# Attention products on half-height tiles, and a local and a strided group taken together

## The chip, the cores and the metric

The kernel runs on one core of a Trainium2 chip. The metric is the device time of one execution in microseconds (us). Before the change it is 878.13 us, the median of 3 runs (877.97 to 878.93).

## The reference

The program computes sparse attention and then a feed-forward layer on its result. There are 8 images of 8 heads, 576 tokens and 64 values per head.

```python
scores = scale * np.matmul(q, k.transpose(0, 1, 3, 2))
mask_local = (rel >= 0) & (rel < stride)            # heads 0 to 3, stride 32
mask_strided = (rel >= 0) & (pos[None, :] % stride == pos[:, None] % stride)   # heads 4 to 7
scores = np.where(masks[None, :, :, :], scores, -1000000000.0)
...
attn = attn / (np.sum(attn, axis=-1, keepdims=True) + 1e-09)
x = (attn @ v) in rows of tokens, 4608 x 512
h = x @ w_in                                       # 512 -> 2048
return ((h * (1.0 / (1.0 + np.exp(-h)))) @ w_out)  # 2048 -> 512
```

A local head sees the 32 tokens up to its own, a strided head the tokens at its own place modulo 32, at most 18 of them. So each score matrix is a set of small blocks.

## The kernel before

**The feed-forward layer.** Each fp32 operand is split in two fp32r parts, and three of the four products are formed on TensorE. A product of this kind has 128 rows of weights, 128 weight columns and 512 moving columns; the text calls it a big product. The first three blocks of 512 tokens are computed directly (`hidden` at L591, `output` at L638). The last six blocks go in three pairs with a Strassen scheme of seven products (L1386 for the hidden layer, L1424 for the output), whose weight operands are formed during blocks 1 and 2 (`prepare`) and kept in DRAM.

**The attention.** A head pair lies in the 128 partitions. Its blocks are cut into six groups per image: three local ones of 12 tiles (32 query rows, 64 keys) and three strided ones of 8, 8 and 6 tiles (64 rows that hold three residues of 18 tokens). A group goes through these steps, with the letters that the planner uses:

- S, scores (L440): one fp32 matmul per tile over all 128 partitions. Its moving operand is `kbd`, which holds the keys of one head beside zeros and zeros beside the other's, so that 2 x 64 columns come out for the two heads.
- M (`peak`, L456, VectorE): mask, scale and row maximum, two instructions for each column of 128 queries. A local group has 3 such columns, a strided one 4, 4 or 3.
- E (L465, ScalarE): the exponential with its row sum, also two for each column. For the first images it is one subtraction on GpSimd (U) and one exponential.
- R (`total`), the reciprocal of the sums, and for strided groups N (`scale`, L489), the scaling of the weights, both on VectorE.
- T (L495): the transposes on TensorE, then P (L499), ScalarE's copy out of PSUM.
- O, values: L507 for local groups (result with queries in the partitions) and L515 for strided ones (result with the head's values in the partitions), with `vbd`, again a block next to zeros.
- Local groups then take Q (`share`, L525, scaling on VectorE) and B, the turn into columns of x: 16 transposes of 32 x 96 on VectorE (L561), or for images 0 and 1 transposes on TensorE (X, L545) and a copy. Strided groups are copied by ScalarE (L538).

**PSUM.** In blocks 0 to 2 the pool `ps` has 4 buffers of one bank, shared by the attention and the hidden layer, and `ps_o` 4. In the Strassen pairs the attention has the 2 buffers of `ps1`, the products `z` 6 banks.

**The order of work.** A planner in the file (class `Steps`) sets the order of the instructions on each engine. Each step has a cost on the engines that may run it, rings of buffers that it takes, and a due time. `arrange` places step by step the one that can start first, and among those that can start within 0.05 us of it the one with the earliest due time. Image 0 comes before the feed-forward layer. Image 1 runs during block 0 on due times of its own. The groups of the other images run at places in a table: `burst(c)` puts T of group c + 1, S of group c + 2 and O of group c at one place.

Of the kernel before, what the change touches and what calls it, by code (L numbers as in the profile page):

```python
# [26 lines left out]
STRIDE = 32  # L27
# [19 lines left out]
KBUFS = 2  # L47
VBUFS = 2
# [25 lines left out]
class Group:  # L74
    def __init__(self, local, first, count):
        self.local, self.first, self.count = local, first, count
        self.rows = STRIDE if local else KW
        self.per = P // self.rows
        self.n = count // self.per
        step = STRIDE if local else SEQ  # L80
        self.q0 = [step * t for t in range(count)]
        half = S // STRIDE
        gap = [STRIDE if local and first < half <= first + t else 0 for t in range(count)]
# [156 lines left out]
def sparse_attention_ffn(ctx: ExitStack, tc: tile.TileContext, kqt, vt, w_in, w_out, out, out_t):  # L240
# [8 lines left out]
    ps = early.enter_context(tc.tile_pool(name="ps", bufs=8 - NTT, space=PSUM))  # L249
    ps_o = early.enter_context(tc.tile_pool(name="ps_o", bufs=NTT, space=PSUM))  # L250
    banks = {"att": ps}
# [5 lines left out]
        (1, 0, 9): "vbd2", (1, 1, 9): "zeros", (1, 0, 7): "kbd2",  # L257
# [6 lines left out]
    vbds = [const.tile([P, 2, VT * D], F32, name=f"vbd{i}") for i in range(VBUFS + 1)]  # L264
    kbds = [const.tile([P, 3, QW], F32, name=f"kbd{i}") for i in range(KBUFS + 1)]
    const.tile([P, 64], F32, name="pad1")
    zeros = const.tile([P, VT * D], F32, name="zeros")
# [5 lines left out]
    nc.vector.memset(kbds[0][:, 0], 0.0)  # L273
    nc.gpsimd.memset(kbds[0][:, 2], 0.0)
    nc.vector.memset(kbds[1][:, 0:3:2], 0.0)
    nc.vector.memset(vbds[0], 0.0)
    nc.vector.memset(zeros, 0.0)
    nc.vector.memset(kbds[2][:, 0:3:2], 0.0)
    for vbd in vbds[1:]:
        for h in range(2):  # L280
            nc.scalar.copy(out=vbd[:, h], in_=zeros)
    vbds = [vbd.rearrange("p h (t d) -> p h t d", d=D) for vbd in vbds]


# [107 lines left out]
    def load_qk(b, gi):  # L392
        n = max(GROUPS[gi].nq, GROUPS[gi].nk)
        for h in range(2):
            load(out=kbds[gi % (KBUFS if b else KBUFS + 1)][h::2, h : h + 2, :n],
                 in_=kqt[b, gi, h::2, :, :n])

    def load_v(b, gi):
        n = GROUPS[gi].count
        for h in range(2):  # L400
            load(out=vbds[gi % (VBUFS if b else VBUFS + 1)][h::2, h, :n], in_=vt[b, gi, h::2, :n])

# [9 lines left out]

    class Attention:


        def __init__(self, b, gi):
            self.b, self.gi, self.g = b, gi, GROUPS[gi]
            g = self.g
            self.kbd = kbds[gi % (KBUFS if b else KBUFS + 1)]
            self.vbd = vbds[gi % (VBUFS if b else VBUFS + 1)]  # L420
            self.cols = g.n * P
            self.tiles = [
                (t, t // g.per, slice(t % g.per * g.rows, (t % g.per + 1) * g.rows))
                for t in range(g.count)
            ]

            self.quick = NG * b + gi < 2 * NG + 2

        def bank(self, name):

            if self.b == 0 and name != "pss":
                return ps_o.tile([P, 512], F32, name="po")
            return banks["att"].tile([P, 512], F32, name="ps")

        def scores(self):
            g, kbd = self.g, self.kbd
            self.pss = self.bank("pss")
            s_ps = self.pss.rearrange("p (c h k) -> p c h k", h=2, k=KW)
            for t, c, rows in self.tiles:
                nc.tensor.matmul(  # L440
                    s_ps[rows, c], kbd[:, 1, g.q0[t] : g.q0[t] + g.rows],
                    kbd[:, 0:3:2, g.k0[t] : g.k0[t] + KW], start=True, stop=True,
                )

        def peak(self):
            g = self.g
            s_ps = self.pss.rearrange("p (c h k) -> p c h k", h=2, k=KW)
            self.sm = att.tile([P, 512], F32, name="sm", bufs=3)
            self.s_sb = s_sb = self.sm.rearrange("p (c k h) -> p c h k", h=2, k=KW)
            sums = att.tile([P, 4, 4, 2], F32, name="sums", bufs=4)  # L450
            self.nmax, self.rsum = nmax, rsum = sums[:, 0], sums[:, 1]
            self.inv = rsum[:, : g.n].unsqueeze(3).broadcast_to([P, g.n, 2, KW])
            for c in range(g.n):
                for h in range(2):

                    nc.vector.tensor_tensor_reduce(  # L456
                        out=s_sb[:, c, h], in0=s_ps[:, c, h],
                        in1=masks[g.local, g.starts[c]][:, :KW],
                        scale=-SCALE, scalar=BIG, op0=ALU.add, op1=ALU.min,
                        accum_out=nmax[:, c, h : h + 1],  # L460
                    )

        def exp_one(self, c):
            for h in range(2):
                nc.scalar.activation(  # L465
                    out=self.s_sb[:, c, h], in_=self.s_sb[:, c, h], func=AF.Exp,
                    bias=self.nmax[:, c, h : h + 1], scale=-1.0,
                    accum_out=self.rsum[:, c, h : h + 1],
                )

        def below(self):
            s_sb = self.s_sb[:, : self.g.n]
            peak = self.nmax[:, : self.g.n].unsqueeze(3).broadcast_to([P, self.g.n, 2, KW])
            nc.gpsimd.tensor_sub(s_sb, peak, s_sb)

        def exp(self):
            sm = self.sm[:, : self.cols]
            nc.scalar.activation(out=sm, in_=sm, func=AF.Exp)

        def total(self):  # L480
            rsum, s_sb = self.rsum[:, : self.g.n], self.s_sb[:, : self.g.n]
            if self.quick:
                nc.vector.tensor_reduce(out=rsum, in_=s_sb, op=ALU.add, axis=mybir.AxisListType.X)
# [3 lines left out]
        def scale(self):  # L487
            s_sb = self.s_sb[:, : self.g.n]
            nc.vector.tensor_mul(s_sb, s_sb, self.inv)  # L489

        def turn(self):
            self.psp = self.bank("psp")
            for c in range(self.g.n):
                at = slice(c * P, (c + 1) * P)
                nc.tensor.transpose(self.psp[:, at], self.sm[:, at], ident)  # L495

        def turned(self):
            self.pt = att.tile([P, 512], F32, name="pt")
            nc.scalar.copy(out=self.pt[:, : self.cols], in_=self.psp[:, : self.cols])  # L499

        def values(self):
            g, pt, vbd = self.g, self.pt, self.vbd
            self.pso = pso = self.bank("pso")
            if g.local:
                o_ps = pso.rearrange("p (c h d) -> p c h d", h=2, d=D)
                for t, c, rows in self.tiles:
                    nc.tensor.matmul(  # L507
                        o_ps[rows, c], pt[:, c * P + rows.start : c * P + rows.stop], vbd[:, :, t],
                        start=True, stop=True,
                    )  # L510
                return
            for t, c, rows in self.tiles:
                p0 = c * P + rows.start
                for h in range(2):
                    nc.tensor.matmul(  # L515
                        pso[h * D : (h + 1) * D, t * SEQ : (t + 1) * SEQ], vbd[:, h, t],
                        pt[:, p0 : p0 + SEQ], start=True, stop=True,
                    )

        def share(self):  # L520
            g = self.g
            self.xq = att.tile([P, 3 * P], F32, name="xq", bufs=1)
            o_ps = self.pso.rearrange("p (c h d) -> p c h d", h=2, d=D)
            o_sb = self.xq.rearrange("p (c h d) -> p c h d", h=2, d=D)
            nc.vector.tensor_mul(o_sb[:, : g.n], o_ps[:, : g.n], self.inv)  # L525

        def sorted(self):
            g, pso = self.g, self.pso

            places = STRIDE + 1  # L530
            at, end = 3 * g.first, 3 * (g.first + g.count)
            while at < end:
                hp, r = divmod(at, places)
                n = min(end - at, STRIDE - r)
                s0 = at - 3 * g.first
                src = pso[:, s0 * NJ : (s0 + n) * NJ].rearrange("p (r j) -> p r j", j=NJ)
                dst = place_of(self.b)[:, NP // 2 + hp].rearrange("p (j r) -> p r j", r=STRIDE)
                nc.scalar.copy(out=dst[:, r : r + n], in_=src)  # L538
                at += n + (r + n == STRIDE)

        def back(self):
            self.psx = self.bank("psp")
            for c in range(self.g.n):
                at = slice(c * P, (c + 1) * P)
                nc.tensor.transpose(self.psx[:, at], self.xq[:, at], ident)  # L545

        def done(self):
            flat = place_of(self.b).rearrange("p n s -> p (n s)")
            x0 = self.g.first * STRIDE
            nc.scalar.copy(out=flat[:, x0 : x0 + self.cols], in_=self.psx[:, : self.cols])  # L550

        def blocks_of(self, t):

            g, n = self.g, P // STRIDE
# [1078 lines left out]
```

## Time and profile before

| what | value |
| --- | --- |
| median of the runs | 878.13 us |
| the profiled execution | 881.13 us |
| its span, first to last instruction | 879.3 us |
| granted TensorE clock | 0.994 |
| busy: TensorE, VectorE, ScalarE, GpSimd | 852.1, 615.0, 467.0, 119.3 us |
| DMA | 180.32 MB, 205 GB/s on average |

The page gives for each engine its busy time and for groups of instructions the busy time, the mean of one, the idle time before them and what ended it. A matmul of two fp32 operands stands in the trace as two products. Lines such as L440 are lines of the kernel printed above.

### The profile page before, as it was taken

Reading aid. Unit: us, or ns where it says so; the run is one execution under the profiler, and the core shown is the slowest. Engines: PE = TensorE matmul, PEld = TensorE weight load, DVE = VectorE, ACT = ScalarE, POOL = GpSimd, SP = SyncE. Lnnn points to the kernel's source line nnn. Section 1 sums busy time; section 2 is a strip of 40 time slices with the busy share of each in tenths; the row PEclk is TensorE's granted clock in tenths of the full one; section 3 lists DMA queues with packets and bytes.
Section 4 is the critical chain, followed back from the end, with each engine's and each line's share of the span. In section 5 each row is a group of like instructions: output and inputs, shape, how many; then the busy total and the mean of one; then the engine's idle time right before and its main releaser. Section 6 shows DMA issues by size and latency. Waiting matters only on the chain.

```text
span 879.3 us, 15187 instructions
## 1 busy us (share of the span) xinstructions
PE 852.1 (97%) x5554; PEld 684.6 (78%) x5554; DVE 615.0 (70%) x1608; ACT 467.0 (53%) x1006; POOL 119.3 (14%) x136
## 2 busy tenths in 40 slices
PE   6799999999999999999999999999999999999997
PEld 4677777778878878777788777787888878888886
DVE  7899757984896797738399975935895660178662
ACT  4888554445456445456754654647554434455440
POOL 4000115332444335200000000000000000000000
PEclk9899999999999999999999999999999999999999
DMA  7897886666444455555655765764546565554562
GB/s 220 297 289 244 241 254 211 226 207 191 141 141 171 140 189 185 189 204 201 228 193 183 244 218 194 259 231 165 194 153 252 194 234 212 196 192 150 218 244 107
DMA packets 79626, 180.32 MB, mean 205 GB/s; under 512 B 7872, under 2 KB 56000, under 8 KB 68800
## 3 DMA queue, kind: packets, MB, share of 16 engines
q1 hardware_dynamic: 79552, 179.35, 60.1%
q8 instruction: 44, 0.72, 0.3%
q14 instruction: 30, 0.25, 0.1%
HBM read 140.53 MB, written 38.80 MB: 204 GB/s over the span
## 4 chain that ended last, share of the span: by engine, by line
PE 73%; DVE 13%; DMA 7%; ACT 3%; POOL 2%; issue 2%; SPq 0%; POOLq 0%; ACTq 0%; DVEq 0%
PE z L1386 26%; PE z L1424 25%; PE po L638 7%; PE ps L591 7%; PE ps L440 4%; DMA stage<-w_in 2%; PE ps L515 2%; DMA w<-ops 2%; DVE g L618 2%; DVE xb L561 2%; DVE w L561 1%; PE ps L495 1%; DVE sm L456 1%; DVE th L605 1%; DMA kbd<-kqt 1%
## 5 line engine op out<-in xcount | busy, mean ns | idle before, releaser
L1386 PE MATMUL z<-w,w 128*128 128x512 f32 x720 | 168.5, 392 | 1.4 <-DMA w<-ops 0.7
L1386 PEld LDWEIGHTS z<-w,w 128*128 128x128 f32 x720 | 134.2, 188 | 31.4 <-issue 1.1
L1424 PE MATMUL z<-w,w 128*128 128x512 f32 x576 | 136.3, 391 | 0.5 <-DMA w<-ops 0.5
L591 PE MATMUL ps<-xhi,w 128*128 128x512 f32 x384 | 131.1, 399 | 2.3 <-ACT pt L499 1.4
L1424 PEld LDWEIGHTS z<-w,w 128*128 128x128 f32 x576 | 107.4, 188 | 24.0 <-DMA w<-ops 1.0
L591 PEld LDWEIGHTS ps<-xhi,w 128*128 128x128 f32 x384 | 72.0, 188 | 21.0 <-issue 1.7
L465 ACT ACTIVATE sm<-sm,sums 128x64 f32<-128x64 f32 x228 | 77.3, 345 | 15.3 <-DVE sums L456 15.2
L591 PE MATMUL ps<-xlo,w 128*128 128x512 f32 x192 | 75.0, 391 | 0.2 <-DVE xlo L583 0.2
L638 PE MATMUL po<-w,g 128*128 128x512 f32 x276 | 71.2, 393 | 0.5 <-DVE g L618 0.4
L638 PEld LDWEIGHTS po<-w,g 128*128 128x128 f32 x276 | 51.2, 188 | 12.6 <-DVE g L618 2.1
L601 ACT ACTIVATE th<-ps 128x512 f32<-128x512 f32 x48 | 28.6, 596 | 49.5 <-PE ps L591 35.3
L440 PE MATMUL ps<-kbd 128*32 128x128 f32 (+1 forms) x928 | 48.4, 294 | 6.5 <-POOL mask_strided L287 5.6
L561 DVE STREAM_TRANSPOSE xb<-xq 32x96 f32<-32x96 f32 x192 | 51.7, 269 | 3.0
L1424 PE MATMUL z<-xhi,w 128*128 128x512 f32 x216 | 52.6, 392 | 0.0
L1424 PE MATMUL z<-xlo,w 128*128 128x512 f32 x216 | 52.6, 392 | 0.0
L1255 DVE TENSOR_TENSOR w<-w,w 128x1024 fp32r<-128x1024 f32 (+3 forms) x41 | 44.9, 1105 | 8.2 <-ACT w L1326 8.1
L440 PEld LDWEIGHTS ps<-kbd 128*32 128x32 f32 (+1 forms) x928 | 35.5, 126 | 18.7 <-issue 10.3
L961 POOL TENSOR_TENSOR stage<-w,w 128x512 f32<-128x512 f32 x23 | 34.7, 1512 | 96.3 <-DMA ops<-stage 70.7
L1424 PEld LDWEIGHTS z<-xlo,w 128*128 128x128 f32 x216 | 40.2, 188 | 8.8 <-issue 0.5
L1424 PEld LDWEIGHTS z<-xhi,w 128*128 128x128 f32 x216 | 40.1, 188 | 8.4 <-issue 0.2
L605 DVE SCALAR_TENSOR_TENSOR th<-th,ps 128x512 f32<-128x512 f32 x48 | 32.5, 677 | 19.1 <-ACT th L601 18.9
L618 DVE TENSOR_TENSOR g<-th,g 128x512 fp32r<-128x512 f32 x48 | 43.8, 912 | 1.7 <-ACT g L614 0.8
(172 smaller groups left out, 1459.0 us busy)
## 6 DMA issues: line engine op xcount, KB each, us to landing
w<-ops SPq DMA_DIRECT2D x84, 1024.0 KB, 4.8
ops<-stage SPq DMA_DIRECT2D x64, 256.0 KB, 2.3
vbd<-vt SPq DMA_DIRECT2D x48, 192.0 KB, 3.6
ops<-w SPq DMA_DIRECT2D x65, 128.0 KB, 3.8
stage<-w_in SPq DMA_DIRECT2D x16, 512.0 KB, 5.2
stage<-w_out SPq DMA_DIRECT2D x16, 512.0 KB, 5.5
kbd<-kqt SPq DMA_DIRECT2D x32, 221.0 KB, 3.9
kbd<-kqt SPq DMA_DIRECT2D x32, 208.0 KB, 3.2
```

The costliest lines, as they stand in the source:

```text
L440: nc.tensor.matmul(s_ps[rows, c], kbd[:, 1, g.q0[t] : g.q0[t] + g.rows], kbd[:, 0:3:2, g.k0[t] : g.k0[t] + KW], start=True, stop=True,)
L465: nc.scalar.activation(out=self.s_sb[:, c, h], in_=self.s_sb[:, c, h], func=AF.Exp, bias=self.nmax[:, c, h : h + 1], scale=-1.0, accum_out ...
L561: nc.vector.transpose(out=dst[cols, :, rows], in_=src[rows, :, cols])
L591: nc.tensor.matmul(ph, weight(0, wi, fc)[:, cc * P : (cc + 1) * P], x[xi][:, cc], start=(cc, n) == (0, 0), stop=(cc, n) == (NP - 1, 2),)
L601: nc.scalar.activation(out=th[:, cols], in_=ph[:, cols], func=AF.Tanh, scale=0.5)
L605: nc.vector.scalar_tensor_tensor(out=th[:, cols], in0=th[:, cols], scalar=1.0, in1=ph[:, cols], op0=ALU.add, op1=ALU.mult,)
L618: nc.vector.tensor_sub(out=g[1][:, cols], in0=th[:, cols], in1=g[0][:, cols].bitcast(F32))
L638: nc.tensor.matmul(po[tt], g[gi][:, cols], weight(1, wi, fc), start=fc == 0 and n == 0, stop=fc == NFC - 1 and n == 2,)
L961: nc.gpsimd.tensor_add(raw[:, 2 * n : 2 * n + 2].rearrange("p a q -> p (a q)"), weight(layer, 0, fc).bitcast(F32), weight(layer, 1, fc).bi ...
L1255: nc.vector.tensor_tensor(out=o, in0=x, in1=y, op=op1)
L1386: nc.tensor.matmul(zt[z][:, jj], w[:, at, wi, cc * P : (cc + 1) * P], op[:, xi, cc], start=fresh and (cc, n) == (0, 0), stop=(cc, n) == (1 ...
L1424: nc.tensor.matmul(zt[zz][:, ds], w[:, at, wi, ds * P : (ds + 1) * P], op[:, gi, jj], start=fresh and (jp, jj, n) == (0, 0, 0), stop=(jp, ...
```

## The change

Each head's product stands alone on 64 rows of the array, head 0 in partitions 0 to 63 and head 1 in 64 to 127, so the zeros beside the blocks and the instructions that wrote them are gone (`kds`, `vds`, three buffers each). The values are formed with the head's values in the partitions, for local groups too; two index bits per product choose the half of the array (`r`) and the half of the result (`r ^ b`), and the host turns the halves of q, k and v to match. ScalarE copies the result straight into x, so `share`, `back`, `done` and `blocks_of` go, and the weights of local groups are scaled before the values as those of strided groups are.

For images 1 to 7 a local and a strided group form one step of 7 (or 6) columns. Scores, transposes and values take the new pool `ps_a`: one buffer of two banks, one bank for each head or each group. The hidden layer keeps 2 buffers, the output 4 banks. The places of S, T and O in the table are now apart from each other. A second `upper` buffer is added in `prepare`, and three weight tiles that shared memory with `kbd`, `vbd` and `zeros` have their own.

```diff
-KBUFS = 2
-VBUFS = 2
+KBUFS = 3
+VBUFS = 3
...
-    ps = early.enter_context(tc.tile_pool(name="ps", bufs=8 - NTT, space=PSUM))
-    ps_o = early.enter_context(tc.tile_pool(name="ps_o", bufs=NTT, space=PSUM))
+    ps_a = ctx.enter_context(tc.tile_pool(name="ps_a", bufs=1, space=PSUM))
+    ps = early.enter_context(tc.tile_pool(name="ps", bufs=6 - NTT, space=PSUM))
+    ps_o = early.enter_context(tc.tile_pool(name="ps_o", bufs=NTT // 2, space=PSUM))
...
         def scores(self):
-            for t, c, rows in self.tiles:
-                nc.tensor.matmul(
-                    s_ps[rows, c], kbd[:, 1, g.q0[t] : g.q0[t] + g.rows],
-                    kbd[:, 0:3:2, g.k0[t] : g.k0[t] + KW], start=True, stop=True,
-                )
+            for g, c0, k in zip(self.gs, self.c0, self.k):
+                kd = kds[k]
+                for t in range(g.count):
+                    rows = slice(t % g.per * g.rows, (t % g.per + 1) * g.rows)
+                    at = (c0 + t // g.per) * KW
+                    for r in range(2):
+                        half = slice(r * D, (r + 1) * D)
+                        nc.tensor.matmul(
+                            self.pss[rows, r, at : at + KW],
+                            kd[half, 1, g.q0[t] : g.q0[t] + g.rows],
+                            kd[half, 0, g.k0[t] : g.k0[t] + KW], start=True, stop=True,
+                        )
...
         def values(self):
+            for g, c0, v in zip(self.gs, self.c0, self.v):
+                wide = STRIDE if g.local else SEQ
+                for t in range(g.half):
+                    for b in range(2):
+                        tile_ = b * g.half + t
+                        q0 = c0 * P + tile_ * g.rows
+                        for r in range(2):
+                            half, to = (slice(x * D, (x + 1) * D) for x in (r, r ^ b))
+                            at = base + t * wide
+                            nc.tensor.matmul(
+                                self.pso[to, b, at : at + wide], vds[v][half, tile_],
+                                self.pt[half, q0 : q0 + wide], start=True, stop=True,
+                            )
...
+        def placed(self, i):
+            if g.local:
+                nc.scalar.copy(
+                    out=flat[:, x0 : x0 + 2 * n].rearrange("p (b n) -> p b n", b=2),
+                    in_=self.pso[:, :, base : base + n],
+                )
...
-    groups = [Attention(b, gi) for b in range(B) for gi in range(NG)]
+    groups = [Attention(0, (gi,)) for gi in range(NG)]
+    groups += [Attention(b, (gi, gi + NG // 2)) for b in range(1, B) for gi in range(NG // 2)]
...
-    for i, at in enumerate([(1, fc) for fc in (0, 2, 4, 5, 7, 9, 11, 12, 14)]
-                           + [(2, fc) for fc in (0, 1, 3, 5, 6, 8, 9, 11, 12)]):
-        plan[at] = 2 * NG + i
+    for i in range(3 * NG // 2):
+        for what, c, at in (("V", i, 3.55 * i), ("T", i + 1, 3.55 * i + 1.2), ("S", i + 2, 3.55 * i + 2.4)):
+            k, fc = divmod(int(at), NFC)
+            plan.setdefault((k + 1, fc), []).append((what, ahead + c))
```

How the order of the instructions changes is shown at three places. A row names the line, the operation, what it writes and reads, the shape, and how often it stands in a row.

TensorE in the first Strassen pair, before: L1386 are big products, L495 transposes, L440 scores, L507 values of a local group.

```order
L1386 MATMUL z<-w_4_4062,w_9_3960 128x512 x24
L495 MATMUL ps<-ident,sm 128x128 x3
L440 MATMUL ps<-kbd_82 32x128 x12
L1386 MATMUL z<-w_8_4058,w_12_4145 128x512 x12
L507 MATMUL ps<-vbd_79,pt 32x128 x12
...
L495 MATMUL ps<-ident,sm 128x128 x3
L440 MATMUL ps<-kbd_83 64x128 x8
L1386 MATMUL z<-xhi,w_5_4258 128x512 x12
L507 MATMUL ps<-vbd_80,pt 32x128 x12
```

The same place now: L1325 are big products, L481 transposes, L425 scores, L503 values.

```order
L1325 MATMUL z<-w_8_4196,w_12_4364 128x512 x24
L481 MATMUL pa<-ident,sm 128x128 x7
L1325 MATMUL z<-xhi,w_5_4517 128x512 x24
L425 MATMUL pa<-kd_83 32x64 x24
L425 MATMUL pa<-kd_84 64x64 x12
L1325 MATMUL z<-w_0_3431,w_9_4549 128x512 x24
L503 MATMUL pa<-pt,vd_87 64x32 x24
L503 MATMUL pa<-pt,vd_85 64x54 x16
L1325 MATMUL z<-w_4_4217,w_12_4573 128x512 x24
```

Scores and values of a local and a strided group now stand together, with twice as many matmuls for each group, half as many moving columns, and 24 big products between neighbouring steps where 12 stood.

VectorE in block 1, before, behind the scores of a local group: L456 is M, L525 is Q, L484 and L485 are R, L561 the transposes into x.

```order
L456 ISA sm,sums<-ps,mask_local 128x64
L456 ISA sums 128x1
L525 TENSOR_TENSOR xq<-ps,sums 128x384
L484 TENSOR_SCALAR sums<-sums 128x6
L485 RECIPROCAL sums<-sums 128x6
L561 STREAM_TRANSPOSE xb<-xq 32x3x32 x12
L456 ISA sm,sums<-ps,mask_strided 128x64
```

VectorE in block 1 now, behind the scores of a pair: L443 is M, L577, L586 and L590 belong to the hidden layer, L470 and L471 are R, L474 is N.

```order
L443 ISA sm,sums<-pa,mask_strided 128x64
L443 ISA sums 128x1
L577 SCALAR_TENSOR_TENSOR th<-th,ph 128x512
L586 CAST g<-th 128x512
L590 TENSOR_TENSOR g<-th,g 128x512
L470 TENSOR_SCALAR sums<-sums 128x14
L471 RECIPROCAL sums<-sums 128x14
L577 SCALAR_TENSOR_TENSOR th<-th,ph 128x512
L474 TENSOR_TENSOR sm<-sm,sums 128x896
```

The scaling of the values and the transposes are gone; one R and one N serve both groups.

TensorE at the start, image 0, before: the letters are those above, L545 is X.

```order
L440 MATMUL ps<-kbd_82 32x128 x12
L440 MATMUL ps<-kbd_83 32x128 x12
L440 MATMUL ps<-kbd_84 32x128 x12
L495 MATMUL po<-ident,sm 128x128 x6
L507 MATMUL po<-vbd_79,pt 32x128 x12
L440 MATMUL ps<-kbd_82 64x128 x8
L545 MATMUL po<-ident,xq 128x128 x3
```

The start now:

```order
L425 MATMUL pa<-kd_82 32x64 x24
L425 MATMUL pa<-kd_83 32x64 x24
L425 MATMUL pa<-kd_84 32x64 x24
L425 MATMUL pa<-kd_82 64x64 x16
L481 MATMUL po<-ident,sm 128x128 x6
L503 MATMUL po<-pt,vd_85 64x32 x24
L425 MATMUL pa<-kd_83 64x64 x16
```

Image 0 keeps its six single groups; the fourth group's scores come ahead of the first transposes, all scores share the one buffer of `pa`, and the turn back (X) is gone.

More of the change, by code (lines that the diff above doesn't have):

```diff
@@ L82, in __init__ @@
         half = S // STRIDE
-        gap = [STRIDE if local and first < half <= first + t else 0 for t in range(count)]
+        self.half = count // 2
+        gap = [STRIDE if local and t >= self.half else 0 for t in range(count)]
         self.k0 = [q0 + g for q0, g in zip(self.q0, gap)]
@@ L411, in place_of, with __init__ @@
         return xs[b]
+    turn_k, turn_v = itertools.count(), itertools.count()
     class Attention:
[L416 to L427, printed above, removed]
+        def __init__(self, b, gis):
+            self.b, self.gis = b, gis
+            self.gs = [GROUPS[gi] for gi in gis]
+            self.c0 = [sum(g.n for g in self.gs[:i]) for i in range(len(gis))]
+            self.n = sum(g.n for g in self.gs)
+            self.k = [next(turn_k) % KBUFS for _ in gis]
+            self.v = [next(turn_v) % VBUFS for _ in gis]
+            self.quick = b < 2
@@ L487, in scale @@
         def scale(self):
-            s_sb = self.s_sb[:, : self.g.n]
-            nc.vector.tensor_mul(s_sb, s_sb, self.inv)
+            nc.vector.tensor_mul(self.s_sb, self.s_sb, self.inv)
         def turn(self):
             self.psp = self.bank("psp")
[L493 to L499, printed above, removed]
@@ L520, in share @@
[L520 to L528, printed above, removed]
-            places = STRIDE + 1
[L531 to L539, printed above, removed]
@@ L641, in output, with new_po @@
                 )
+    def new_po():
+        tiles_ = [ps_o.tile([P, 2, DM], F32, name="po") for _ in range(NTT // 2)]
+        return [t[:, i] for t in tiles_ for i in range(2)]
     def store(k, po):
@@ new lines, in add_total @@
+    def add_total(c, t0=None):
+        if c >= len(groups):
+            return
+        a = groups[c]
+        due = None if t0 is None else t0 - 1.5
+        parts = [f"sm{c}.{j}" for j in range(a.n)]
+        do(f"R{c}", {"DVE": 0.45 + (0.15 * a.n if a.quick else 0.0)}, a.total, reads=parts,
+           writes=[f"sum{c}"], due=due)
+        r = do(f"N{c}", {"DVE": 0.08 + 0.14 * a.n}, a.scale, reads=[f"sum{c}"], writes=parts,
+               due=None if due is None else due + 0.5)
+        steps.ends(steps[f"M{c}.0"], "sum", [r])
@@ new lines, in add_values @@
+    def add_values(c, t0=None):
+        a = groups[c]
+        after = (lambda d: None) if t0 is None else (lambda d: t0 + d)
+        ring = "po" if a.b == 0 else "pa"
+        for g, gi, v in zip(a.gs, a.gis, a.v):
+            do(f"v{c}.{gi}", {"SP": P * g.count * D * 4 / RATE}, lambda gi=gi, v=v: load_v(a.b, gi, v),
+               writes=[f"vd{v}"], due=after(-5))
+        o = do(f"O{c}", {"PE": 0.3 + sum(0.7 if g.local else 0.5 for g in a.gs)}, a.values,
+               reads=[f"vd{v}" for v in a.v] + [f"pt{c}.{i}" for i in range(len(a.gs))],
+               writes=[f"pso{c}"], takes=[ring], due=after(0))
+        steps.ends(steps[f"P{c}.0"], "pt", [o])
+        made = []
+        for i, (g, gi) in enumerate(zip(a.gs, a.gis)):
+            x = do(f"B{c}.{i}", {"ACT": 0.5 if g.local else 1.0}, lambda i=i: a.placed(i),
+                   reads=[f"pso{c}"], due=after(1 + i / 2))
+            outs_of[a.b, gi] = [x]
+            made.append(x)
+        steps.ends(o, ring, made)
+        return made
```

438 lines of the change are left out of this document (181 added, 257 removed).

## The prediction

> **What bounds the kernel now.** I read the page's engine rows and slices first, then the stretches, then who TensorE waits for, and last the chain of waits around single attention steps.
>
> ```profile
> PE 852.1 (97%) x5554; PEld 684.6 (78%) x5554; DVE 615.0 (70%) x1608; ACT 467.0 (53%) x1006; POOL 119.3 (14%) x136
> ...
> PE   6799999999999999999999999999999999999997
> ...
> PEclk9899999999999999999999999999999999999999
> ...
> PE 73%; DVE 13%; DMA 7%; ACT 3%; POOL 2%; issue 2%; SPq 0%; POOLq 0%; ACTq 0%; DVEq 0%
> ```
>
> TensorE is busy in every slice from the second on, at full clock. The chain of waits puts only 73% on it, but a chain also goes back through work that was on time by design. So I ask TensorE itself, by stretch and by wait:
>
> ```profile
> 115.00:366.00 251.00, 246.43 (x1839) 197.83 (x1839) 197.63 (x642) 122.66 (x392) 102.08 (x99) 1.00 0.57 184
> 366.00:642.00 276.00, 274.69 (x1798) 219.54 (x1799) 189.19 (x533) 164.72 (x368) 0.00 (x0) 0.99 0.60 210
> 642.00:880.00 238.00, 231.48 (x1067) 190.52 (x1065) 135.54 (x127) 99.87 (x107) 0.00 (x0) 1.00 0.54 195
> ```
>
> ```profile
> PE po L638 <- DVE g L618: 3.2, 4, 1.6
> PE ps L507 <- DVE th L605: 1.4, 1, 1.4
> ...
> PE po L638 <- DVE g L614: 0.3, 1, 0.3
> ```
>
> Columns of the first: window, length, then busy time of PE, PE's weight loads, DVE, ACT, POOL. From 115 to 642 us TensorE is busy 521.1 of 527 us. The second lists all its waits from 44 us to the end: ten rows from 3.2 down to 0.3 us, 9.3 us in all. The kernel is therefore a queue of TensorE work, and what an attention step takes there, with the break it makes in the big products, is what it costs. Such steps stand in the chain like this (start, length, what; the trace counts two products for one fp32 matmul of the program, so 24 are 12 tiles):
>
> ```profile
> 506.39 2.77 PE z L1424 x12
> 509.16 0.81 PE ps L440 x12
> 509.96 2.96 PE z L1424 x12
> 512.93 1.07 PE ps L515 x32
> ...
> 519.68 0.33 PE ps L495 x3
> 520.01 2.75 PE z L1424 x12
> 522.77 0.79 PE ps L440 x24
> 523.56 1.07 PE ps L515 x32
> 524.63 2.96 PE z L1424 x12
> ```
>
> ```profile
> 385.17 0.79 PE ps L507 x24
> ...
> 389.25 1.02 PE ps L440 x16
> ...
> 659.88 0.84 PE ps L515 x24
> ...
> 721.60 76.44 PE z L1386 x336
> ```
>
> Undisturbed, 12 big products take 76.44/28 = 2.73 us; behind scores or values they take 2.96. Call that **re-entry, 0.23 us** a break. Transposes cost none: 2.75 follows the 0.33. Scores take 0.79 (local), 1.02 (strided, 8 tiles), 0.81 (6 tiles); values 0.79 (local), 1.07 and 0.84.
>
> What sets 0.79 and 1.07 is seen by closing a window a little later each time and counting the products begun (last field; windows from 381.36 to 381.40, .48, .52, .63, then from 410.20 to 410.23, .285, .345):
>
> ```profile
> 381.36 0.32 PE L440 MATMUL ps<-kbd 128*32 128x128 f32 x4
> 381.36 0.42 PE L440 MATMUL ps<-kbd 128*32 128x128 f32 x8
> 381.36 0.54 PE L440 MATMUL ps<-kbd 128*32 128x128 f32 x12
> ...
> 410.08 0.33 PE L515 MATMUL ps<-pt,vbd 128*64 128x54 f32 x4
> 410.08 0.39 PE L515 MATMUL ps<-pt,vbd 128*64 128x54 f32 x6
> 410.08 0.45 PE L515 MATMUL ps<-pt,vbd 128*64 128x54 f32 x8
> ```
>
> The four 32-row column tiles begin together (x4 at .40, still x4 at .48, x8 at .52, x12 at .63): **rounds of four, about 0.11 us apart**, for 128 moving columns. 0.79 is six such rounds (0.66) and 0.13 to fill and leave. For the values (54 columns, two column tiles) a round of two comes every 0.058 us, while 54 columns at the pace of 128 would need 0.11 x 54/128 = 0.046. There the load of 64 weight columns sets the round.
>
> **The change, part by part.**
>
> *Products.* The zero half of each operand goes. A tile's two heads become two products over 64 rows each, one in the upper and one in the lower half of the array. A local group issues 48 traced products for its scores instead of 24, with 64 moving columns instead of 128, and 8 array tiles can hold them at once; a strided one 32 instead of 16, with 4 tiles. Values: 48 (32 columns) instead of 24, and 32 (54 columns) as now, both on 4 tiles instead of 4 and 2. The trace has no product on 64 rows, so whether the halves run side by side is bounded from both sides.
> - Side by side: local scores 48/8 = 6 rounds of 0.055 (half of 0.11), 0.33; strided 32/4 = 8 rounds of 0.058, 0.46; 0.13 to fill and leave; between 32-wide and 64-wide tiles a switch that I set at 0.1 (nothing at least, a re-entry, 0.23, at most). Scores 1.02, values (12 + 8) x 0.058 + 0.13 = 1.29. A pair with 6 strided tiles saves two rounds in each: 0.90 and 1.17.
> - One after the other: 12 x 0.055 + 16 x 0.058 + 0.23 = 1.82 for scores and (24 + 16) x 0.058 + 0.13 = 2.45 for values; 1.59 and 2.22 with 6 tiles.
>
> I take side by side, because column tiles, the nearest thing in the trace, do begin within 0.04 us of each other. The Trainium skill, "TensorEngine Tiling (Array Packing)", section "Key Properties", says the same of row tiles: different tiles load and multiply in parallel. It also says that a change of tiling drains the engine, which the 0.23 us agrees with.
>
> *Breaks.* Between the first big product and the end the order of before has 63 breaks with scores or values in them, that of the change 42 (21 pairs, two each). Transposes keep their number and cost.
>
> *The sum on TensorE*, for the 21 pairs of images 1 to 7, 14 with 8 and 7 with 6 strided tiles:
> - before: 21 x (0.79 + 0.79) + 14 x (1.02 + 1.07) + 7 x (0.81 + 0.84) = 74.0; 63 x 0.23 = 14.5; three turn-backs of image 1 at 0.33 each, 1.0. Together 89.5.
> - after: 14 x (1.02 + 1.29) + 7 x (0.90 + 1.17) = 46.8; 42 x 0.23 = 9.7. Together 56.5, **33 us less**. One after the other it would be 14 x 4.27 + 7 x 3.81 + 9.7 = 96.2, 7 us more.
> - If the weight loads did not set the round at all, local values would fall to 12 x 0.11 x 32/128 = 0.33 from 0.70, and strided work by 0.012 a round: 21 x (0.37 + 0.19) = 12 us more saved. That is the lower bound.
>
> *Readers.* These lie beside TensorE:
>
> ```profile
> L561 DVE STREAM_TRANSPOSE xb<-xq 32x96 f32<-32x96 f32 x192 | 51.7, 269 | 3.0
> L525 DVE TENSOR_TENSOR xq<-ps,sums 128x384 f32<-128x384 f32 x21 | 11.6, 552 | 6.2 <-PE ps L507 6.2
> L489 DVE TENSOR_TENSOR sm<-sm,sums 128x384 f32<-128x384 f32 x8 | 5.6, 701 | 0.2
> L538 ACT COPY xb<-ps 128x432 f32<-128x432 f32 x5 | 4.9, 972 | 1.9 <-PE ps L515 1.9
> L499 ACT COPY pt<-ps 128x384 f32<-128x384 f32 x28 | 13.3, 475 | 12.2 <-PE ps L495 12.2
> L499 ACT COPY pt<-ps 128x512 f32<-128x512 f32 x14 | 8.2, 589 | 8.3 <-PE ps L495 8.3
> 8.82 0.14 DVE sm L456
> DVE sm L456 <- PE ps L440: 40.5, 18, 12.1
> ```
>
> A local group of images 2 to 7 loses 16 transposes (16 x 0.269 = 4.3 us) and the 0.55 scaling of its values on VectorE, and gains at most 0.70 for scaling its weights: 18 x 4.1 = 75 us of VectorE's 615 go. None of it is in the sum, since TensorE hides it today. It pays only through the 9.3 us of waits, nearly all on VectorE; I count 3 us back, with 0 and 9 as ends. ScalarE gains a copy of about 0.48 per local group and some cuts in the strided copies, under 1 us a pair and 20 in all, in an engine idle for 47%.
>
> *Bank pairs.* Scores, transposes and values of images 1 to 7 now share one pair of PSUM banks, so each must wait until the last one's readers are through: 14 reductions x 0.14 = 2.0 us after scores, 0.475 + 0.589 = 1.06 after transposes, some 2 after values. Before there were several buffers. On TensorE's in-order queue a late reader holds the big products behind the step, and their VectorE and ScalarE work after them. The cover is 12 to 24 big products (2.73 to 5.46 us) between most neighbours. I allow 5 us for the few places with 12 (0 and 20 as ends); the rival below is what it costs without cover.
>
> *DMA and the start.* Key and value loads keep their bytes with half the issues, so SP's queue is no longer than now.
>
> ```profile
> 5.58 2.99 PE ps L440 x48
> ...
> 9.28 1.51 PE ps L440 x24
> ...
> PE po L515 <- ACT pt L499: 3.0, 1, 3.0
> ```
>
> In the start the first three score steps run almost together today, with buffers to spare; on one bank pair each waits for six reductions (0.9 us) and a hand-over, at most 4 us later. Against that the zero fills go, and with ScalarE's four zero copies perhaps its 3.0 us hold on the values. I take 0, with -3 and +4 as ends.
>
> Sum: -33 - 3 + 5 + 0 = **-31 us**. The profiled execution took 881.1 us (span 879.3), 3.0 over the median of the runs, 878.1. So 850 for a profiled execution like it, and **847 us** for the median.
>
> **Rivals.**
> 1. *The halves do not run side by side.* For: no row shows 64-row tiles. Against: four products on distinct tiles begin within 0.04 us, twelve within 0.27. Price: +7, with the 2 of the other terms 878.1 + 9 = **887, slower**. It decides from about 2.1 us per step upward, where products and breaks cost what they do today. The Trainium skill has a rule with this outcome, in "TensorE: Matmul & The Clock Gate", section "Wait — 56ns, not 53.3ns?": start to start never falls below about 25 ns however short the product. By it 80 products would take 80 x 0.025 = 2.0 us a step, an estimate from that page, and the saving would be gone. The four starts within 0.04 us disagree with it for distinct tiles.
> 2. *Waits at the single bank pair.* 63 uses after the start. Each late by 0.7 us on average gives 44 us: 878.1 - 36 + 44 = **886, slower**; break-even at 36/63 = 0.57 us. For: the step's work on VectorE and ScalarE is now in one piece of twice the size. Against: VectorE sat waiting for scores 18 times (40.5 us), so readers are mostly there first.
> 3. *Half of it.* Row tiles share the weight-load path in part, or waits eat 15 to 20 us: **865**, between the bounds above. Nothing in the trace is against it but the starts.
> 4. *The start or the weights hold image 0.* If TensorE's time saved before 115 us (three pairs, 5 us) meets weights that are not there yet, the result is **852**; the waits list has no DMA wait of that stretch, so little speaks for it.
>
> **How the numbers follow.** Forecast, with rival 4 as its upper part: 0.72, its own range 835 to 857 (lower bound 847 - 12; above, waits of 15 instead of 5). Rival 3: 0.11. Rival 1: 0.09. Rival 2: 0.06. The last 0.02 is a still faster one. About 0.2% (1.8 us) is what a measurement can tell from no change. Faster: 0.72 + 0.02 + 0.11 + 0.01 of rivals 1 and 2 = 0.86; of what is left 0.03 falls within 0.2% and 0.11 above. For 8 in 10 the range takes in the forecast and rival 3's middle: 835 to 868.
>
> **What would show it.** Right: score steps of a pair near 1.0 us and value steps near 1.3 in the chain of waits, the big products behind them still 2.95; local score products beginning eight to a round; VectorE's busy time down by some 75 us; TensorE's waits after 44 us under 15 us; big products at 2.73 per 12. Wrong: steps of 1.8 and 2.4 us (rival 1); a list of waits in which transposes wait for VectorE or scores for ScalarE with tens of us (rival 2); a first big product later than 36 us (the start).

## Result, and the profile after the change

| | before | after |
| --- | --- | --- |
| median | 878.53 us (4 runs, 877.97 to 880.81) | 849.84 us (4 runs, 846.44 to 851.07) |
| the profiled execution | 881.13 us | 846.44 us |
| its span | 879.3 us | 844.7 us |
| granted TensorE clock | 0.994 | 0.998 |

After to before the ratio is 0.9662, 95% interval 0.9627 to 0.9698: 28.7 us less in the medians, 34.7 between the two profiled executions. Before's profiled execution lies 2.6 over its median, after's 3.4 under, which is the 6 us between these two numbers; single terms below come from the traces, verdicts from the medians.

The engine rows of the page, and the shares of the chain of waits:

```profile
PE 820.5 (97%) x7040; PEld 669.1 (79%) x7040; DVE 529.5 (63%) x1257; ACT 462.5 (55%) x1051; POOL 117.6 (14%) x130
...
PE 89%; DVE 5%; DMA 2%; ACT 2%; issue 1%; POOL 1%; ACTq 0%; DVEq 0%; POOLq 0%
```

TensorE issues 1486 products more and is busy 31.6 us less. VectorE lost 85.5 us (75 were expected); ScalarE, which was expected to gain, lost 4.5. TensorE is still busy 97% of the span, and its share of the chain rose from 73 to 89%: the kernel is the same queue, with less in it. All that TensorE waits for from 40 us to the end, 7.0 us (the same question gave 9.3 from 44 us on before):

```profile
PE po L610 <- DVE g L590: 3.1, 3, 2.1
PE ph L563 <- DVE th L577: 2.1, 1, 2.1
PE po L610 <- ACT g L586: 0.5, 1, 0.5
PE pa L503 <- PE z L1363: 0.5, 1, 0.5
PE z L1325 <- DMA w<-ops: 0.4, 1, 0.4
PE ph L563 <- DVE xlo L555: 0.2, 1, 0.2
PE pa L425 <- ACT pt L487: 0.2, 1, 0.2
```

Only the last row is a wait for a reader of the bank pair that scores, transposes and values now share. Single steps in the chain of waits of after (L425 scores, L503 values, L1325 and L1363 big products; x77 and x69 are steps of 80 and 72 products, of which the chain leaves a few out):

```profile
375.05 1.16 PE pa L425 x69
...
381.88 1.32 PE pa L503 x80
...
394.99 1.28 PE pa L425 x77
396.27 8.40 PE z L1325 x36
...
404.67 1.20 PE pa L503 x72
...
499.80 1.28 PE pa L425 x77
501.08 2.98 PE z L1363 x12
...
686.96 76.44 PE z L1325 x336
```

A pair's values take 1.32 us, its scores 1.28; with six strided tiles 1.20 and 1.16. The big products behind a break still take 2.98 per 12 against 76.44/28 = 2.73 undisturbed. Inside the score step at 394.99, the timeline with its window closed a little later each time (at 395.05, .16, .24, .41 and .60), as the prediction read that of before:

```profile
394.92 0.34 PE L425 MATMUL pa<-kd 64*32 64x64 f32 x16
394.92 0.46 PE L425 MATMUL pa<-kd 64*32 64x64 f32 x32
394.92 0.48 PE L425 MATMUL pa<-kd 64*32 64x64 f32 x33
394.92 0.69 PE L425 MATMUL pa<-kd 64*32 64x64 f32 x46
394.92 0.94 PE L425 MATMUL pa<-kd 64*32 64x64 f32 x52
```

32 products have begun 0.24 us into the step: eight per 0.056 us as forecast, so both halves of the array work at once. Then there is a pause (one more product in the next 0.08 us), and the last sixteen local products need 0.27 us where two rounds would be 0.11. After the switch to 64-wide tiles the single records of the trace put the eighth strided product 0.27 us behind the last local one, and the remaining 24 in 0.35 us: rounds of four per 0.058 us.

### The profile page after: what moved, and what is told of

The parts are those of the page before. It is cut to its first block, busy times and chain, and to the rows that moved or that the text cites. A ratio compares the mean times of both kernels' runs of the same rounds, so it can differ in the third digit from the quotient of the medians.

```text
span 844.7 us, 17679 instructions
## 1 busy us (share of the span) xinstructions
PE 820.5 (97%) x7040; PEld 669.1 (79%) x7040; DVE 529.5 (63%) x1257; ACT 462.5 (55%) x1051; POOL 117.6 (14%) x130
## 4 chain that ended last, share of the span: by engine, by line
PE 89%; DVE 5%; DMA 2%; ACT 2%; issue 1%; POOL 1%; ACTq 0%; DVEq 0%; POOLq 0%
PE z L1325 27%; PE z L1363 26%; PE po L610 13%; PE ph L563 13%; PE pa L425 3%; PE pa L503 3%; PE pa L481 1%; DVE xlo L555 1%; PE po L503 1%; DMA w<-ops 1%; DMA stage<-w_out 1%; DMA ops<-stage 1%; PE po L481 1%; ACT sm L452 0%; DVE sm L443 0%
## 5 line engine op out<-in xcount | busy, mean ns | idle before, releaser
L1325 PE MATMUL z<-w,w 128*128 128x512 f32 x720 | 167.6, 391 | 0.5 <-DMA w<-ops 0.4
L1325 PEld LDWEIGHTS z<-w,w 128*128 128x128 f32 x720 | 134.3, 188 | 29.7 <-ACT w L1076 0.8
L1363 PE MATMUL z<-w,w 128*128 128x512 f32 x576 | 136.2, 391 | 0.0
L563 PE MATMUL ph<-xhi,w 128*128 128x512 f32 x384 | 132.2, 404 | 2.2 <-DVE th L577 2.1
L1363 PEld LDWEIGHTS z<-w,w 128*128 128x128 f32 x576 | 107.5, 188 | 22.6
L610 PE MATMUL po<-w,g 128*128 128x512 f32 x432 | 104.6, 391 | 0.1
L563 PEld LDWEIGHTS ph<-xhi,w 128*128 128x128 f32 x384 | 72.6, 189 | 18.9 <-DVE th L577 3.0
L1195 DVE TENSOR_TENSOR w<-w,w 128x1024 fp32r<-128x1024 f32 (+3 forms) x68 | 77.7, 1151 | 13.5 <-ACT w L1266 11.0
L563 PE MATMUL ph<-xlo,w 128*128 128x512 f32 x192 | 75.6, 394 | 0.9 <-DVE xlo L555 0.9
L577 DVE SCALAR_TENSOR_TENSOR th<-th,ph 128x512 f32<-128x512 f32 x48 | 32.9, 686 | 51.3 <-ACT th L573 51.1
L1224 DVE TENSOR_TENSOR w<-w,z 128x1024 f32<-128x1024 f32 x30 | 36.6, 1219 | 39.2 <-PE z L1325 39.1
L1266 ACT CAST w<-w 128x1024 fp32r<-128x1024 f32 (+1 forms) x40 | 39.2, 987 | 35.1 <-PE z L1363 32.9
L1212 ACT ACTIVATE w<-w 128x1024 f32<-128x1024 f32 x30 | 31.8, 1061 | 37.2 <-DVE w L1224 36.9
L1363 PE MATMUL z<-xlo,w 128*128 128x512 f32 x216 | 52.1, 390 | 0.0
L1363 PE MATMUL z<-xhi,w 128*128 128x512 f32 x216 | 51.9, 389 | 0.0
L1218 ACT COPY w<-z 128x1024 f32<-128x1024 f32 x30 | 30.4, 1013 | 33.9 <-PE z L1325 33.9
L1363 PEld LDWEIGHTS z<-xhi,w 128*128 128x128 f32 x216 | 40.5, 188 | 8.4
L1363 PEld LDWEIGHTS z<-xlo,w 128*128 128x128 f32 x216 | 40.4, 188 | 8.4
```

Source lines behind the costliest of these rows:

```text
L563: nc.tensor.matmul(ph, weight(0, wi, fc)[:, cc * P : (cc + 1) * P], x[xi][:, cc], start=(cc, n) == (0, 0), stop=(cc, n) == (NP - 1, 2),)
L577: nc.vector.scalar_tensor_tensor(out=th[:, cols], in0=th[:, cols], scalar=1.0, in1=ph[:, cols], op0=ALU.add, op1=ALU.mult,)
L610: nc.tensor.matmul(po[tt], g[gi][:, cols], weight(1, wi, fc), start=fc == 0 and n == 0, stop=fc == NFC - 1 and n == 2,)
L1195: nc.vector.tensor_tensor(out=o, in0=x, in1=y, op=op1)
L1212: nc.scalar.activation(out=o, in_=x, func=AF.Silu)
L1224: nc.vector.tensor_add(o, x, y)
```

## Experiments

Theory: the halves of the array run side by side, and TensorE's queue pays for products and breaks one for one. Rivals: the products cost little, and what was gained is VectorE's relief or the fewer breaks. All times are compared with runs of the kernel before on the same chip, whose medians were 879.3, 879.5 and 878.9 us.

**1. VectorE's relief alone.** The kernel before, with the 16 transposes of `back` on VectorE replaced by one copy. The turn into columns of x is left out, so that x is not the reference's.

```diff
-            dst = flat.rearrange("p (c q) -> p c q", q=P)
-            for d in range(n):
-                rows, cols = (slice(i * STRIDE, (i + 1) * STRIDE) for i in (t, d))
-                nc.vector.transpose(out=dst[cols, :, rows], in_=src[rows, :, cols])
+            if t == 0:
+                nc.vector.tensor_copy(out=flat, in_=self.xq[:, : self.cols])
```

> The kernel before, with the 16 VectorE transposes that turn a local group into columns of x replaced by one plain copy (so the turn is left out and the result is not the reference's); 18 groups, some 4 us of VectorE time each, 70 us in all. Theory (that time is hidden behind TensorE and pays only through TensorE's 9.3 us of waits): 3 us less, 870 to 879. Rival (VectorE's load is what the change relieved): 15 to 30 us less, 848 to 863.

Measured: 875.36 us (872.58 to 880.09, 10 runs), ratio to before 0.9966 [0.9944, 0.9988]. Its engine row:

```profile
PE 849.9 (97%) x5554; PEld 684.1 (78%) x5554; DVE 550.4 (63%) x1338; ACT 466.9 (53%) x1006; POOL 121.6 (14%) x136
```

64.6 us of VectorE's work go and 3 us of time with them (by the ratio; 3.9 by the medians). VectorE's relief is about a tenth of the gain, as the prediction counted it.

**2. The halves issued apart.** In scores and values the loop over the two halves goes outside the loop over tiles: all products of the upper half first, then those of the lower.

```diff
-                for t in range(g.count):
-                    ...
-                    for r in range(2):
+                for r in range(2):
+                    ...
+                    for t in range(g.count):
```

> The changed kernel, but within each score and value step all products of the upper 64 rows are issued first and then all of the lower 64 rows, so that two halves are neighbours only once in a step; same products, same order of steps. Theory (the gain comes from the row halves running side by side): score steps grow from 1.28 us by about 0.75 and value steps from 1.32 to about 2.45, 1.9 us for each of 21 pairs, so about 40 us more than the change: 884 to 892 us, the gain gone. Rival (the gain comes from fewer breaks and the freed VectorE): within 3 us of the change, 847 to 853.

Measured: 870.67 us (869.57 to 871.16, 4 runs), ratio 0.9905 [0.9881, 0.9929]. That is 20.8 over the change, between the two theories. From the chain of waits, and from the timeline of the score step with the window closed at 413.80, 413.95 and 414.05:

```profile
400.07 1.89 PE pa L503 x79
413.76 1.60 PE pa L425 x72
```

```profile
413.69 0.32 PE L425 MATMUL pa<-kd 64*32 64x64 f32 x8
413.69 0.48 PE L425 MATMUL pa<-kd 64*32 64x64 f32 x27
413.69 0.59 PE L425 MATMUL pa<-kd 64*32 64x64 f32 x36
```

The score step grew from 1.28 to 1.60 (80 products, the chain shows 72) and the values from 1.32 to 1.89, not to 1.82 and 2.45. The last two rows show why: between .95 and .05 nine products begin in 0.10 us, and 19 in the 0.15 us before, where one half alone would give four per 0.058. The records do not name the half, but from the 13th product on a second series of fours stands between the rounds of the first, and 27 starts are more than the 24 local products of the upper half. So products of the lower half, which stand 24 places later in the order, started ahead of upper ones. The edit did not keep the halves apart, and its number is no measure of them.

**3. One half only.** Here nothing is left to overtake: every product takes its operands from rows 0 to 63. Head 1's attention is not computed. Number, sizes and places of the products stay.

```diff
-                        half = slice(r * D, (r + 1) * D)
+                        half, q0 = slice(0, D), g.q0[(t + r) % g.count]
...
-                            half, to = (slice(x * D, (x + 1) * D) for x in (r, r ^ b))
+                            half, to = (slice(x * D, (x + 1) * D) for x in (0, r ^ b))
```

> Edit: every product of scores and values takes its operands from the upper half, rows 0 to 63 (the lower half's product is replaced by one more on the upper half, of the same size, written to the same place); so head 1's attention is not computed, and the output is not the reference's. No two products can stand on different halves, which the run with the halves issued apart left possible. Theory (the halves side by side are what the change gains on the products, and the earlier run lost only half because products of the other half overtook): local scores 12 rounds of 0.058 instead of 48 products in 0.51 us, strided scores 16 rounds of 0.058 instead of 8, values 40 rounds of 0.058 instead of 20; a pair pays about 0.6 us more for scores (1.9 us a step) and 1.1 us more for values (2.45 us a step), 21 x 1.65 = 35 us and some 3 us in image 0: 849.8 + 38 = 888 us, range 880 to 893, so slower than before. Rival (the halves are worth only the 21 us that the earlier run lost, the rest of its forecast was wrong): 868 to 873 us, with steps of 1.6 and 1.9 us as there.

Measured: 891.8 us (889.6 to 894.0, 4 runs), ratio to before 1.0146 [1.0116, 1.0176]: slower than before, 42 us over the change. The chain of waits, and the timeline with the window closed at 426.15, .30 and .55:

```profile
426.04 1.99 PE pa L425 x78
436.43 2.24 PE pa L503 x72
...
471.85 2.47 PE pa L503 x80
...
488.96 1.75 PE pa L425 x70
```

```profile
425.97 0.39 PE L425 MATMUL pa<-kd 64*32 64x64 f32 x12
425.97 0.52 PE L425 MATMUL pa<-kd 64*32 64x64 f32 x21
425.97 0.77 PE L425 MATMUL pa<-kd 64*32 64x64 f32 x38
```

26 products in 0.40 us, about four per 0.06. 14 pairs at 1.99 + 2.47 instead of 1.28 + 1.32 and 7 at 1.75 + 2.24 instead of 1.16 + 1.20 make 14 x 1.86 + 7 x 1.63 = 37.5 us; the first big product starts 8.0 us later (36.3 for 28.3). Together that is 45.5, where the two profiled executions lie 43.2 apart. The theory holds, the rival's 868 to 873 does not. Without the second half the change would have lost: the twice as many products are paid for only because two halves take them at once.

**4. Scores issued twice.** The same results are written twice.

```diff
-            for g, c0, k in zip(self.gs, self.c0, self.k):
+            for g, c0, k in list(zip(self.gs, self.c0, self.k)) * 2:
```

> The changed kernel with the products of every score step issued twice (the second set writes the same numbers again). Theory (TensorE is a full queue, every microsecond of an attention step is paid): 21 steps grow by 1.15 us less for 6 tiles, with one more change of tile width each; 23 to 27 us more than the change, 873 to 877 us. Rival (part of a step lies in waits that it would fill): less than half of it, 850 to 861.

Measured: 881.72 us (880.25 to 887.75, 10 runs), ratio 1.0042 [1.002, 1.0064]; 31.9 over the change, and above the theory's 873 to 877. From the chain:

```profile
399.76 2.33 PE pa L425 x138
...
420.86 2.68 PE pa L425 x154
```

The steps grew by 1.40 and 1.17 us, 14 x 1.40 + 7 x 1.17 = 27.8 for the pairs. Between the 48th big product and the last the trace has 25.4 more, and 9.8 more up to the 48th. This second part is what the theory left out: image 0 has six score steps that run with nothing beside them. In the steps of the pairs the added products are paid nearly one for one, and no wait hides them; the rival falls.

**5. Local and strided part at two places.** Scores and values of a pair stay one piece for VectorE and ScalarE; TensorE does the local part, then 12 big products at most places, then the strided part. `scores` and `values` get an index `i` and the planner a step for each.

```diff
-        def scores(self):
-            self.pss = self.bank("pss")
-            for g, c0, k in zip(self.gs, self.c0, self.k):
+        def scores(self, i):
+            if i == 0:
+                self.pss = self.bank("pss")
+            for g, c0, k in list(zip(self.gs, self.c0, self.k))[i : i + 1]:
...
```

> Edit: the scores and the values of a pair stay one piece for VectorE and ScalarE, but TensorE forms them at two places, the local part first and the strided part after 12 (at some places 6 or 24) big products; the same products, 40 breaks more in all. It undoes the part of the change that puts a local and a strided group at one place. Theory (a break costs 0.23 us of re-entry behind it and 0.13 us to fill and leave, and the joined step pays about 0.1 us to switch the tile width instead): 40 x (0.23 + 0.13) - 40 x 0.1 = 10 us more than the change, 860 us, with 857 to 864 as range; the big products behind each part take 2.95 per 12. Rival (the breaks are nearly free, the gain is in the products alone, or the split even helps because readers start earlier): 846 to 853 us.

Measured: 864.23 us (864.18 to 865.96, 4 runs), ratio 0.9832 [0.9816, 0.9848]; 14.4 over the change. In the timeline L506 are values, L426 scores, L1359 big products. The difference of two starts is what a step takes:

```profile
394.68 0.90 PE L506 MATMUL pa<-pt,vd 64*64 64x32 f32 x48
395.51 3.02 PE L1359 MATMUL z<-w,w 128*128 128x512 f32 x12
398.46 0.69 PE L506 MATMUL pa<-pt,vd 64*64 64x54 f32 x32
399.07 3.02 PE L1359 MATMUL z<-w,w 128*128 128x512 f32 x12
...
405.42 0.72 PE L426 MATMUL pa<-kd 64*32 64x64 f32 x48
406.08 3.02 PE L1359 MATMUL z<-w,w 128*128 128x512 f32 x12
409.02 0.69 PE L426 MATMUL pa<-kd 64*64 64x64 f32 x32
409.65 5.74 PE L1359 MATMUL z<-xhi,w 128*128 128x512 f32 x24
```

Values: 0.83 + 0.61 = 1.44 against 1.32 together. Scores: 0.66 + 0.63 = 1.29 against 1.28 together. So putting the two score parts side by side saves only the re-entry; the switch from 32-wide to 64-wide tiles costs what the second filling of the array would. Counted: 20 score and 19 value breaks, 39 x 0.23 + 19 x 0.12 = 11.3 us, and TensorE's waits from 40 us on are 10.8 us instead of 7.0: 15.1 together. The two profiled executions lie 17.8 apart: in that of the split the clock row shows 0.50 for 3.4 us at 137 us and again at 369 us, and the products there take some 2.9 us longer than at full clock. The theory holds with a result just above its range; the 3.8 us of waits were not in it.

**6. Strided part first, and local scores twice.** Two small runs on the slow last sixteen products of the local scores.

```diff
-            for g, c0, k in zip(self.gs, self.c0, self.k):
+            for g, c0, k in reversed(list(zip(self.gs, self.c0, self.k))):
```

> The changed kernel with the strided group's score products issued ahead of the local group's in the paired steps. In the change the first 32 products of a step begin 0.007 us apart and the last 16 local ones 0.017 us apart, and the step takes 1.28 us where 1.02 was forecast. Theory A (TensorE's queue runs dry after the first 32 products and refills at about 0.017 us a product): with the strided ones first, which take 0.058 us for four anyway, the queue fills again in time, the step takes 1.05 us, 4 to 5 us less than the change in all, 844 to 846. Theory B (the slow third belongs to the end of a run of 32-wide tiles): step and time unchanged, 849 to 851.

Measured: 850.52 us (845.79 to 852.26), ratio 0.9671 [0.9626, 0.9716], no different from the change; the step in the chain:

```profile
396.93 1.28 PE pa L425 x77
```

Theory A falls as it was put. In the trace's records the local part, now last, again has 32 quick products and then sixteen slow ones. That is as Theory B says, which the next run then goes against. The other edit:

```diff
-                for t in range(g.count):
+                for t in [*range(g.count)] * (2 if g.local and len(self.gs) > 1 else 1):
```

> Edit: in the steps of a pair the products of the local scores are issued twice in a row, 96 instead of 48 traced products, then the strided ones as before; the output stays the same. Question: in the change the first 32 local products start about 0.007 us apart and the last 16 about 0.017 us apart. Theory A (TensorE has 32 to some 50 products ready when a step begins and is then fed one product per 0.017 us): the added 48 all come at the slow pace, 48 x 0.017 = 0.8 us more, the step goes from 1.28 to about 2.1 us, and the time to 849.8 + 21 x 0.8 = 867 us. Theory B (only the last 16 products of a run of one width are slow, because the next width waits behind them): the added 48 come at the fast pace, 48 x 0.007 = 0.34 us more, the step is about 1.6 us and the time 857 us. The closing windows over one step tell which: under A 32 to 48 products in the first 0.35 us and a constant 0.017 after that, under B 80 in the first 0.6 us.

Measured, in one run with a profile: 854.82 us, 8.4 over the profiled execution of the change, and steps of 1.73 (and 1.61). From the timeline, window closed at 251.94, 252.10, .30 and .50:

```profile
251.60 0.57 PE L425 MATMUL pa<-kd 64*32 64x64 f32 x35
251.60 0.74 PE L425 MATMUL pa<-kd 64*32 64x64 f32 x51
251.60 0.93 PE L425 MATMUL pa<-kd 64*32 64x64 f32 x71
251.60 1.11 PE L425 MATMUL pa<-kd 64*32 64x64 f32 x92
```

After the first 32 products, 16 in 0.16, 20 in 0.20 and 21 in 0.20 us: a steady **0.010 us** per product, neither A's 0.017 nor B's 0.007. The 48 added products cost 0.45 us, near B's sum. What stands between is a pause of about 0.1 us behind the 32nd product, seen in the score steps of the change and of experiments 4 to 6, and a slower feed from then on. The feed does not follow TensorE's clock: in the score step at 137.6 us of experiment 5, where the clock row shows 0.50, the first 32 products begin within 0.37 us instead of 0.24, the last sixteen within 0.23, and within 0.24 at full clock. The Trainium skill, "TensorE: Matmul & The Clock Gate", section "Architectural detail: the array is 16× 32×32, not 1× 128×128", gives TensorE a queue of 64 entries; 32 products with their 32 weight loads would be that many, which fits the pause. That it is the queue was not shown: no run changed the number of weight loads per product.

## Why the prediction was right, step by step

The forecast was 847 us from a sum of -31; the medians give 849.8 and -28.7, the profiled executions -34.7. The steps:

- *TensorE is a full queue.* Right: added products (4), added rounds (3) and added breaks (5) all arrive in the time nearly one for one. The prediction also says that TensorE ran at full clock from the second slice on; its own clock row has an 8 there, which matters for the start (below).
- *Side by side.* Right. Experiment 3 made the other case real: the 887 us of rival 1 are measured as 891.8, with value steps of 2.47 for 2.45 forecast and score steps of 1.99 for 1.82. The rule that speaks for rival 1, in the Trainium skill, "TensorE: Matmul & The Clock Gate", section "Wait — 56ns, not 53.3ns?" (start to start not below about 25 ns), does not hold across tiles here: 32 products begin within 0.24 us. Rival 3 (half of it, 865) falls with the time, 849.8, and with rounds of eight.
- *The values' round is set by loading 64 weight columns.* The forecast that followed is right, 1.29 against 1.32; the reason is not shown. Local values move 32 columns, strided ones 54; alone, in experiment 5, they took 0.83 and 0.61 us, and 12 rounds of 0.058 with 0.13 are 0.83, 8 are 0.59. The lower bound of the prediction, rounds that shrink with the columns (0.70 to 0.33 for local values), is excluded. But a fixed least time per round would look the same as the weight load, since no step here has fewer than 64 of both weight and moving columns.
- *Scores of a pair 1.02 us.* **This is the term that was mis-sized: 1.28.** Of the 0.26, about 0.18 are local products behind the 32nd, which do not come eight per round (0.51 us from the first to the last of 48 instead of 0.33), 0.06 the width switch (0.16 instead of 0.1; eight strided products after the last local one take 0.27, two rounds are 0.117), and 0.02 the filling. Over 14 pairs, and 7 at 1.16 for 0.90, that is 14 x 0.26 + 7 x 0.26 = 5.5 us.
- *Products and breaks together, -33.* By the rows of after 14 x (1.28 + 1.32) + 7 x (1.16 + 1.20) + 42 x 0.23 = 62.6 instead of 56.5, against 89.5: **-26.9**.
- *Re-entry 0.23, transposes none.* Right: 2.98 and 2.95 behind scores and values, and experiment 5 paid the 0.23 again at each added break.
- *VectorE, -3.* Right: 3.0 alone in experiment 1, and TensorE's waits from the first big product on fell from 10.9 to 7.7.
- *Bank pairs, +5.* Not needed: 0.2 us in the list of waits. The 12 to 24 big products between neighbours cover the readers. Rival 2 falls.
- *The start, 0.* Its parts were both real. TensorE's longest wait in the list of the kernel before up to 45 us:

```profile
PE ps L440 <- POOL mask_strided L287: 5.6, 1, 5.6
```

In the list of after up to 40 us:

```profile
PE pa L425 <- DMA kd<-kqt: 4.2, 1, 4.2
PE pa L425 <- DVE sums L443: 2.3, 2, 1.2
PE po L503 <- ACT pt L487: 1.7, 2, 1.0
```

The first scores wait 4.2 us for their keys, where they waited 5.6 for GpSimd; the hold on the values fell from 3.0 to 1.7; the reductions that must leave the one bank pair cost 2.3. The first big product starts at 28.3 instead of 32.4 us, 4.1 us earlier, past the lower end, -3. How much of this the change did is not shown, because TensorE's clock was not the same in the two starts. Two stretches of before (the third field from the end is the granted clock, before it are the busy times):

```profile
25.10:31.90 6.80, 6.09 (x90) 5.23 (x92) 6.31 (x15) 5.93 (x11) 0.00 (x0) 0.50 1.04 386
366.40:369.90 3.50, 3.50 (x10) 2.73 (x9) 3.03 (x6) 2.73 (x5) 0.00 (x0) 0.51 0.36 132
```

In the second stretch the big products start every 0.43 us and their records last 0.63, instead of 0.23 and 0.39. In the chain of after, the first six big products:

```profile
28.67 2.56 PE ph L563 x6
```

They too start every 0.43 us and last 0.63, where six undisturbed ones need 1.37 us in all. So they fit half the clock, although the clock row, whose records begin at 32.7 us in this trace, reads 1.00 there. The hidden layer then waits 2.1 us for VectorE (L577). At the 48th big product the lead is 1.4 us, at the 96th 0.1 (where the change has the values of a whole pair behind it and the kernel before does not), at the 192nd 5.8, and it grows to 34.6 at the last.
- *Rival 4 (weights hold image 0).* No DMA wait over 0.4 us after 40 us; what held the early blocks was VectorE.

From the first big product to the last the forecast's sum, -31, stands beside -30.6 in the traces: -26.9 by the steps, -3.2 by waits, +1.2 by the slow first six of after, and -1.6 by the second stretch above, where eight big products of before each come 0.2 us late. The last two belong to the clock and not to the change. That this is so near is partly chance, since the score term was 5.5 too low and the allowance for the bank pair 5 too high. The medians moved 6 us less than the profiled executions, which lie at opposite ends of their spreads.

## What to carry to other kernels

Where TensorE is a full queue, count what a step occupies from the first of its starts to the next foreign one, and ask whether smaller tiles that stand beside each other would shorten it. Twice the products on half the rows paid here only because both halves work at once; on one half they lost 13 us against the kernel before. A join of two steps is worth its re-entry, but a change of tile width inside the joined step can cost as much as the filling that it saves. To take one resource away in an experiment, take it out of the operands; a new order of issue was not enough, since products on free tiles overtook.

## What was not expected of the hardware

- Short products on distinct tiles begin 0.007 us apart (32 in 0.24 us), but after 32 of them there is a pause of about 0.1 us and then one per 0.010 us in a longer run. The slower feed is the same at half the clock (experiment 5); the cause is open.
- Products overtake others that stand ahead of them in the order but need a busy half (experiment 2): 27 starts within 0.26 us, where one half alone gave 21 in 0.33 (experiment 3).
- A switch from 64x32 to 64x64 tiles costs some 0.16 us, as much as ending one step and filling the next (0.66 + 0.63 apart, 1.28 joined). The Trainium skill, "TensorEngine Tiling (Array Packing)", section "Key Properties", says that such a change drains the engine; the trace fits that, with 0.146 us between the last local start and the first strided one.
- The round of four 64-wide products takes 0.058 us whether 64, 54 or 32 columns move.
